# The first projected block of an MLP set in a fixed order on TensorE, VectorE and ScalarE

## The chip, the cores and the metric

One core of one Trainium2 chip runs the whole program. The metric is the device time of one execution in microseconds (us), as the median of several runs. TensorE (PE) multiplies matrices into PSUM, VectorE (DVE) and ScalarE (ACT) do the elementwise work and move results out of PSUM, and the queue of SyncE (SP) issues nearly all transfers.

## The reference

In short form (softmax(t, n) is over axis n). Three stages follow each other; the change lies at the beginning of the third. Attention with 48 heads gives x, a soft mixture of experts turns it into slots and combination weights, and an MLP follows:

```python
def _moe_ref(x, phi, w1, w2):
    logits = x @ phi                       # (1792, 32)
    slot_input = softmax(logits, 0).T @ x  # 32 slots of 768
    for e in range(8):
        slot_out[e] = relu(slot_input[e] @ w1[e]) @ w2[e]
    return softmax(logits, 1) @ slot_out

def _moe2_ref(x, w_in, w_out, alpha):
    h = x @ w_in                           # (1792, 768) @ (768, 2048)
    g = np.maximum(h, 0.0) + alpha * np.minimum(h, 0.0)
    return (g @ w_out).astype(np.float32)  # (1792, 2048) @ (2048, 768)
```

The arrays w_in and w_out come as float64, and the kernel turns them into float32 itself.

## The kernel before

Since the mixture's output is a combination of 32 slots, the kernel never forms it: it multiplies the 32 slot outputs (tile so) with w_in, which gives a_stk, and gets each hidden activation from a_stk and the combination weights (cstk) in one product. Numbers are kept in a high and a low part for TensorE's fast format; a part's product is taken three times (high by high, high by low, low by high).

The third stage begins when the last expert's product y stands in PSUM:

- `gather` (from L907) copies y out (ysb), transposes it (yt) and copies it twice into so. `idle` puts products of the identity (warm) where TensorE would have nothing to do.
- `a_block(fb, lo, w)` (from L925) makes columns of a_stk: 12 products in the two column halves of TensorE (aps), which the profile counts as 24, then for each half j a ScalarE copy of the high part (L950) and a VectorE subtraction for the low part (L951). Block 0 is made in two column blocks of 256 columns, the others whole.
- `hidden(tb, f)` (from L959) is the hidden row f of token block tb, 128 of the 2048 hidden units for 512 tokens: one product (hps, L962), two ReLUs on ScalarE (L968, L969), the weighted sum on VectorE (L970), the high part on ScalarE (L978) and the low part on VectorE (L979), in the tiles gs and gr. For the very first row VectorE does both halves of the activation itself (L974, L977).
- `to_single(f)` (from L816) converts row f of w_out from float64 to float32 with `to_f32` (L192): Abs on ScalarE (L194), then four operations on VectorE (L195, L199, L202, L205). `split_wo(f)` (from L826) splits it into high (ScalarE, L837) and low part (VectorE, L838), the tile wsp.
- `project(tb, f, tiles)` (from L994) multiplies a hidden row with its row of w_out into six PSUM banks: 24 products for a block of 512 tokens, 12 of them 512 wide and 12 256 wide (L1002, L1008, L1009; tile oc).

A main loop goes over 16 rows f for token block 0, then for block 1, and the four other blocks come after it in another form. Every engine runs its instructions strictly in the order in which they stand. That order is not the order of the code: a scheduler orders them by priorities and modelled times, and a manual dependency without a semaphore ("NOSYNC") only forces one instruction to stand behind another. PSUM tiles ps_w have two buffers, ps_c six. All transfers of weights stand in one queue in the order of their use.

```python
            hidden_to(1)
            idle(2, warm)
            hidden_to(2)
            a_block(0, 256, 128)

            for n, (tb, f) in enumerate(units):
                ...
                hidden_to(n + 3)
                ...
                project(tb, f, range(blocks[tb][1] // 128))
```

## Time and profile before

| | us |
|---|---|
| median of 3 runs | 587.15 |
| the three runs | 588.32, 585.62, 587.15 |
| the profiled execution | 587.28 |
| its span, first to last instruction | 585.0 |
| PE busy in the span | 553.1 (95%) |
| DVE busy | 435.1 (74%) |
| ACT busy | 377.6 (65%) |

The profile's page gives busy times for the whole span. The change concerns the stretch from about 327 us, where the last expert ends, to about 345 us, and through the order of the instructions the 100 us behind it. Times inside the span are counted from its first instruction. Consecutive matmuls overlap in the profile, so that the distance from start to start is what one costs, not its duration.

### The profile page before, as it was taken

What the parts mean: (1) busy time and instruction counts of PE and PEld (TensorE: products, weight loads), DVE (VectorE), ACT (ScalarE), POOL (GpSimd) and SP (SyncE); (2) the same over time, 40 slices, a digit from 0 to 9 for tenths busy, and PEclk for the clock granted to TensorE, in tenths of its full rate; (3) what the DMA queues carried; (4) which work ended last, traced back from release to release, by engine and by line L of the source; (5) the groups of instructions that cost most, each with busy time, mean ns of one, the idle gap of its engine ahead of it and who ended that gap; (6) DMA issues with size and microseconds to landing.
All of it is one profiled execution on the core that took longest, in us unless ns stands there. A gap on an engine that the chain in (4) does not pass through costs nothing.

```text
span 585.0 us, 10832 instructions
## 1 busy us (share of the span) xinstructions
PE 553.1 (95%) x4030; PEld 384.7 (66%) x4030; DVE 435.1 (74%) x834; ACT 377.6 (65%) x617; POOL 173.9 (30%) x158
## 2 busy tenths in 40 slices
PE   5999999999999999998888799999999999999996
PEld 4444444445444545464445577878888999999996
DVE  3878777796999768460023489999999979797974
ACT  3999999898889788530011266854777755555551
POOL 0789788676785755500000000000000000000000
PEclk9999999999999999999999999999999999999999
DMA  7668789987787971999999999200120101010101
GB/s 174 155 141 251 230 263 269 266 255 200 225 256 214 326 229 53 350 347 418 416 417 419 390 404 414 111 1 1 55 55 1 55 1 54 2 55 0 55 2 54
DMA packets 83460, 110.92 MB, mean 190 GB/s; under 512 B 55376, under 2 KB 63312, under 8 KB 81872
## 3 DMA queue, kind: packets, MB, share of 16 engines
q1 hardware_dynamic: 81168, 109.28, 55.3%
q10 hardware_dynamic: 2240, 0.95, 0.6%
q8 instruction: 32, 0.52, 0.4%
q14 instruction: 20, 0.16, 0.1%
HBM read 98.41 MB, written 11.80 MB: 188 GB/s over the span
## 4 chain that ended last, share of the span: by engine, by line
PE 71%; DMA 14%; ACT 8%; DVE 5%; issue 2%; SPq 1%; ACTq 0%
PE o L295 10%; DMA w<-in_moe_w_dram 9%; PE s L295 8%; PE P L1229 7%; PE P L1227 7%; PE P L1228 7%; PE oc L1002 6%; PE oc L1008 6%; PE oc L1009 6%; DMA v<-in_v_dram 3%; ACT p L398 2%; PE aps L930 2%; ACT p L397 2%; PE nx L295 2%; PE rs L295 2%
## 5 line engine op out<-in xcount | busy, mean ns | idle before, releaser
L295 PE MATMUL o<-p,v 128*64 128x448 f32 (+1 forms) x384 | 93.3, 564 | 5.8 <-ACT xu L423 3.7
L397 ACT ACTIVATE p<-s 128x896 f32<-128x896 f32 x96 | 78.7, 821 | 21.1 <-PE s L295 18.0
L398 ACT ACTIVATE p<-p,cap 128x896 f32<-128x896 f32 x96 | 90.9, 949 | 2.3
L414 POOL TENSOR_TENSOR acc<-p 128x448 f32<-128x448 f32 x48 | 62.1, 1313 | 55.6 <-ACT p L398 55.6
L1008 PE MATMUL oc<-wsp,gr 128*128 128x512 f32 (+1 forms) x192 | 65.3, 341 | 0.0
L1009 PE MATMUL oc<-wsp,gr 128*128 128x512 f32 (+1 forms) x192 | 64.1, 337 | 0.0
L1002 PE MATMUL oc<-wsp,gr 128*128 128x512 f32 (+1 forms) x192 | 62.6, 343 | 0.0
L295 PEld LDWEIGHTS s<-qh,kh 64*128 64x128 f32 (+1 forms) x168 | 18.1, 185 | 66.5 <-issue 25.6
L1218 ACT ACTIVATE gr<-gs 128x384 fp32r<-128x384 f32 (+1 forms) x64 | 36.7, 576 | 32.8 <-DVE gs L1202 26.9
L417 POOL TENSOR_TENSOR acc<-acc,p 64x448 f32<-64x448 f32 x46 | 55.4, 1204 | 1.7
L421 POOL TENSOR_TENSOR acc<-acc,p 128x448 f32<-128x448 f32 x46 | 53.5, 1183 | 1.8
L1219 DVE TENSOR_TENSOR gr<-gs,gr 128x384 fp32r<-128x384 f32 x64 | 39.2, 620 | 17.4 <-ACT gr L1218 17.4
L295 PE MATMUL s<-qh,kh 64*128 64x448 f32 (+1 forms) x168 | 45.8, 473 | 0.0
L1227 PE MATMUL P<-wsp,gr 128*128 128x384 f32 x128 | 42.9, 335 | 0.0
L1229 PE MATMUL P<-wsp,gr 128*128 128x384 f32 x128 | 42.8, 334 | 0.0
L1228 PE MATMUL P<-wsp,gr 128*128 128x384 f32 x128 | 42.8, 334 | 0.0
L1002 PEld LDWEIGHTS oc<-wsp,gr 128*128 128x128 f32 x192 | 36.6, 192 | 5.6 <-ACT wsp L837 0.8
L1008 PEld LDWEIGHTS oc<-wsp,gr 128*128 128x128 f32 x192 | 36.8, 191 | 5.2 <-DVE wx L205 0.4
L1009 PEld LDWEIGHTS oc<-wsp,gr 128*128 128x128 f32 x192 | 36.3, 189 | 4.4 <-issue 0.4
L295 PEld LDWEIGHTS o<-p,v 128*64 128x64 f32 (+1 forms) x384 | 19.0, 134 | 30.3 <-ACT xu L423 12.3
L295 PE MATMUL s<-ql,kh 64*128 64x448 f32 (+1 forms) x168 | 35.5, 366 | 1.0 <-DVE ql L377 1.0
L295 PE MATMUL s<-qh,kl 64*128 64x448 f32 (+1 forms) x168 | 35.5, 365 | 0.0
(237 smaller groups left out, 1227.3 us busy)
## 6 DMA issues: line engine op xcount, KB each, us to landing
w<-in_moe_w_dram SPq DMA_DIRECT2D x26, 768.0 KB, 12.4
w<-in_moe_w_dram SPq DMA_DIRECT2D x12, 1536.0 KB, 12.2
cvbuf<-in_moe_w_in_dram SPq DMA_DIRECT2D x24, 512.0 KB, 5.4
w<-in_moe_w_out_dram SPq DMA_DIRECT2D x16, 768.0 KB, 11.1
w_in<-cvbuf SPq DMA_DIRECT2D x24, 256.0 KB, 2.8
w<-in_moe_w_dram SPq DMA_DIRECT2D x12, 512.0 KB, 7.4
q<-in_q_dram SPq DMA_DIRECT2D x44, 112.0 KB, 3.6
k<-in_k_dram SPq DMA_DIRECT2D x48, 96.0 KB, 4.8
```

The costliest lines, as they stand in the source:

```text
L295: ins = nc.tensor.matmul(*a, **kw)
L397: nc.scalar.activation(out=pe, in_=ps[:, :n, :S], func=AF.Tanh)
L398: nc.scalar.activation(out=pe, in_=pe, func=AF.Exp, scale=cap_sb)
L414: nc.gpsimd.tensor_add(out=a[:, u, :], in0=pt[i, 0][:, u, :], in1=pe[:, u, :])
L417: nc.gpsimd.tensor_add(out=a[r, u, :], in0=a[r, u, :], in1=pt[i, JK][r, 0, :])
L421: nc.gpsimd.tensor_add(out=a[:, u, :], in0=a[:, u, :], in1=pe[:, u, :])
L1002: ins = nc.tensor.matmul(o, gh[:, ts], wo_h[f][:, cols], start=(f == 0 and not second), stop=False)
L1008: nc.tensor.matmul(o, gh[:, ts], wo_l[f][:, cols], start=False, stop=False)
L1009: nc.tensor.matmul(o, gl[:, ts], wo_h[f][:, cols], start=False, stop=(f == KF - 1 and not more))
L1227: nc.tensor.matmul(o, hi[:, i], bh, start=(p == 0), stop=False)
L1228: nc.tensor.matmul(o, hi[:, i], bl, start=False, stop=False)
L1229: nc.tensor.matmul(o, lo[:, i], bh, start=False, stop=(p == 7))
```

## The change

The first block of the third stage gets a fixed order on three engines. A function `follow` chains instructions of ScalarE ("a") and VectorE ("v") to each other, and the matmuls of the block are chained by `pe[0]`.

- Copies in `gather` are divided: VectorE takes the first half of ysb and of so, ScalarE the second.
- `to_f32` ends after the shift; the two last operations are `to_f32_end`. For row 1 of w_out the first part comes ahead of the first column block's copies, the second part behind the first hidden row's activation.
- The first hidden row (`hidden_0`) has a PSUM buffer of its own from ps_c. Its 512 tokens are divided in two halves of 256: VectorE works on the first, ScalarE's two ReLUs on the second. Its low part (`low_0`) follows later, in two halves.
- The second column block's products come right behind the first hidden row's product, its copies (`late_copies`) behind everything of hidden row 1 and of the split of row 1 of w_out.
- `project_0` does the first row's projection in another order and chained behind the matmul that was written before it, which is that of hidden row 2.
- Six warm products of the identity become three.

```diff
-        def to_single(f):
+        def follow(lane, ins, yes=True):
+            if not yes:
+                return ins
+            if lane in turn:
+                tc.add_manual_dep(ins.ins, turn[lane].ins.name, NOSYNC, reason="first block in a fixed order")
+            turn[lane] = ins
+            return ins
+
+        def to_single(f, first=False):
...
-            nc.vector.tensor_copy(out=ysb, in_=yacc[:32 * G3, :256])
+            follow("v", nc.vector.tensor_copy(out=ysb[:, :128], in_=yacc[:32 * G3, :128]))
+            follow("a", nc.scalar.activation(out=ysb[:, 128:], in_=yacc[:32 * G3, 128:256], func=AF.Copy))
...
+                if lo and first:
+                    return copy_out
+                copy_out()
...
+            def hidden_0():
...
+                follow("a", a.activation(out=mn[:, y], in_=ps[:, y], func=AF.Relu, scale=-1.0))
+                follow("v", v.tensor_scalar(
+                    out=mn[:, x], in0=ps[:, x], scalar1=0.0, scalar2=al, op0=ALU.min, op1=ALU.mult
+                ))
+                follow("a", a.activation(out=gf[:, y], in_=ps[:, y], func=AF.Relu))
+                follow("v", v.scalar_tensor_tensor(
+                    out=gf[:, x], in0=ps[:, x], scalar=0.0, in1=mn[:, x], op0=ALU.max, op1=ALU.add
+                ))
+                follow("a", a.activation(out=gh[:, x], in_=gf[:, x], func=AF.Copy))
+                follow("v", v.scalar_tensor_tensor(
+                    out=gf[:, y], in0=mn[:, y], scalar=na, in1=gf[:, y], op0=ALU.mult, op1=ALU.add
+                ))
+                follow("a", a.activation(out=gh[:, y], in_=gf[:, y], func=AF.Copy))
...
+            def project_0():
+                gh, gl = gt[0, 0]
+                for left, right in ((gh, (wo_h[0], wo_l[0])), (gl, (wo_h[0],))):
...
+                                tc.add_manual_dep(
+                                    ins.ins, pe[0].ins.name, NOSYNC, reason="first block in a fixed order"
+                                )
+                                pe[0] = ins
...
-            to_single(1)
-            split_wo(1)
-            a_block(0, 0, 128)
-            idle(4, warm)
...
+            first, then, shift = to_single(1, True)
+            follow("a", first)
+            follow("v", then)
+            follow("v", shift)
+            a_block(0, 0, 128, True)
+            idle(3, warm)
+            hidden_0()
+            late_copies = a_block(0, 256, 128, True)
+            for ins in to_f32_end(where["wo", 0, 0][:, 1], wf[0][1]):
+                follow("v", ins)
+            low_0()
+            steps = hidden(0, 1, True)
+            for _ in range(3):
+                next(steps)
+            split_wo(1, True)
+            for _ in steps:
+                pass
+            late_copies()
+            ready[0] = 2
...
-                project(tb, f, range(blocks[tb][1] // 128))
+                if n == 0:
+                    project_0()
+                else:
+                    project(tb, f, range(blocks[tb][1] // 128))
```

**ScalarE and VectorE from the first column block to the copies of the second.** A wait is named by the engine or the transfer queue (DMAHW) whose semaphore it is on. ScalarE before:

```order
L950 ACTIVATE a_stk<-aps 64x128 [waits DMAHW0_49,DMAHW7_49,PE_49,Pool_49]
L194 ACTIVATE wf<-w 128x768 [waits DMAHW4_49]
L950 ACTIVATE a_stk<-aps 64x128 [waits DVE_49]
L968 ACTIVATE gs<-hps 128x512 [waits DMAHW7_49,DMAHW0_49,PE_49]
L969 ACTIVATE gs<-hps 128x512
```

ScalarE now:

```order
L936 ACTIVATE ysb<-y 96x128 [waits DVE_49]
L947 ACTIVATE so<-yt 128x2x3x32 [waits DMAHW5_49,DVE_49,Pool_49]
L194 ACTIVATE wf<-w 128x768 [waits DMAHW4_49]
L958 ACTIVATE a_stk<-aps 64x128 [waits DMAHW7_49,DMAHW0_49,PE_49]
L958 ACTIVATE a_stk<-aps 64x128 [waits DVE_49]
L1029 ACTIVATE gs<-hps 128x256 [waits DMAHW7_49,DMAHW0_49,PE_49]
L1033 ACTIVATE gs<-hps 128x256 [waits DVE_49]
L1037 ACTIVATE gr<-gs 128x256 [waits DMAHW6_49,DMAHW5_49,DVE_49]
L1041 ACTIVATE gr<-gs 128x256 [waits DVE_49]
```

VectorE's L1030 and L1034, in the same stretch, wait for ScalarE's semaphore in turn. VectorE before, from the first subtraction for a_stk:

```order
L951 TENSOR_TENSOR a_stk<-aps,a_stk 64x128
L974 TENSOR_SCALAR gs<-hps,alpha 128x512
L195 TENSOR_SCALAR wf<-wf 128x768
L951 TENSOR_TENSOR a_stk<-aps,a_stk 64x128
L199 TENSOR_SCALAR wf<-wf 128x768
L977 SCALAR_TENSOR_TENSOR gs<-hps,gs 128x512
L202 SCALAR_TENSOR_TENSOR wf<-w,wf 128x768
L970 SCALAR_TENSOR_TENSOR gs<-gs,nalpha 128x512
L205 SCALAR_TENSOR_TENSOR wf<-w,wf 128x768
L979 TENSOR_TENSOR gr<-gs,gr 128x512 x2
L951 TENSOR_TENSOR a_stk<-aps,a_stk 64x128
```

VectorE now, from behind its copy into so:

```order
L195 TENSOR_SCALAR wf<-wf 128x768
L199 TENSOR_SCALAR wf<-wf 128x768
L959 TENSOR_TENSOR a_stk<-aps,a_stk 64x128 x2
L1030 TENSOR_SCALAR gs<-hps,alpha 128x256
L1034 SCALAR_TENSOR_TENSOR gs<-hps,gs 128x256
L1038 SCALAR_TENSOR_TENSOR gs<-gs,nalpha 128x256
L207 SCALAR_TENSOR_TENSOR wf<-w,wf 128x768
L210 SCALAR_TENSOR_TENSOR wf<-w,wf 128x768
L1048 TENSOR_TENSOR gr<-gs,gr 128x256 x2
L1012 SCALAR_TENSOR_TENSOR gs<-gs,nalpha 128x512
L859 TENSOR_TENSOR wsp<-wf,wsp 128x768
L1016 TENSOR_TENSOR gr<-gs,gr 128x512
```

The next VectorE row now is the pair of subtractions for the second column block. Row 1's Abs and its first two VectorE operations moved ahead of the first column block's copies, and the second column block's subtractions moved behind the split of row 1.

**TensorE from the first column block to the first projection.** Before:

```order
L930 MATMUL aps<-w,so 64x128 x12
L812 MATMUL warm<-ident 128x128 x4
L962 MATMUL hps<-cstk,a_stk 128x512
L812 MATMUL warm<-ident 128x128 x2
L962 MATMUL hps<-cstk,a_stk 128x512
L930 MATMUL aps<-w,so 64x128 x12
L1002 MATMUL oc<-wsp,gr 128x512
L1008 MATMUL oc<-wsp,gr 128x512
```

Nine more projection matmuls follow before the next hps, that of hidden row 2. Now:

```order
L965 MATMUL aps<-w,so 64x128 x12
L820 MATMUL warm<-ident 128x128 x3
L1022 MATMUL hps<-cstk,a_stk 128x512
L965 MATMUL aps<-w,so 64x128 x12
L1002 MATMUL hps<-cstk,a_stk 128x512 x2
L1058 MATMUL oc<-wsp,gr 128x512 x2
L1058 MATMUL oc<-wsp,gr 128x256 x2
```

The product of hidden row 2 (the second of the two hps) now stands ahead of all 24 projection matmuls, where 11 of them stood ahead of it.

**TensorE at column block 1 of a_stk** (the same is seen at blocks 2 and 3). Before:

```order
L930 MATMUL aps<-w,so 64x256 x8
L962 MATMUL hps<-cstk,a_stk 128x512
L930 MATMUL aps<-w,so 64x256 x2
L1002 MATMUL oc<-wsp,gr 128x512
L1008 MATMUL oc<-wsp,gr 128x512
L930 MATMUL aps<-w,so 64x256 x2
L1009 MATMUL oc<-wsp,gr 128x512
```

Now:

```order
L1058 MATMUL oc<-wsp,gr 128x512
L1058 MATMUL oc<-wsp,gr 128x256
L965 MATMUL aps<-w,so 64x256 x12
L1002 MATMUL hps<-cstk,a_stk 128x512
L1086 MATMUL oc<-wsp,gr 128x512
```

The 12 products of the block, which stood in three pieces between others, now stand together.

## Rows read from the trace of the kernel before

**Rows 1.** TensorE in order of time: start, duration, line, output<-inputs, count, idle before.
```profile
331.32 0.47 PE L962 MATMUL hps<-cstk,a_stk 128*128 128x512 f32 x1
...
334.74 2.16 PE L930 MATMUL aps<-w,so 128*64 128x128 f32 x24 [0.82 <-DVE gs L977]
336.83 0.80 PE L1002 MATMUL oc<-wsp,gr 128*128 128x512 f32 x1
...
340.38 0.39 PE L962 MATMUL hps<-cstk,a_stk 128*128 128x512 f32 x1
340.61 0.39 PE L1009 MATMUL oc<-wsp,gr 128*128 128x512 f32 x1
...
342.03 0.28 PE L1008 MATMUL oc<-wsp,gr 128*128 128x256 f32 x1
342.15 0.28 PE L1009 MATMUL oc<-wsp,gr 128*128 128x256 f32 x1
```

**Rows 2.** Stretches: length; busy PE, PEld, DVE, ACT, POOL; granted clock, DMA share, GB/s.
```profile
335.00:336.00 1.00, 1.00 (x18) 1.00 (x16) 1.00 (x2) 0.57 (x2) 0.00 (x0) 0.74 1.01 385
336.00:337.00 1.00, 1.00 (x11) 0.67 (x8) 1.00 (x2) 0.69 (x2) 0.00 (x0) 0.50 1.04 383
...
338.00:339.00 1.00, 1.00 (x4) 0.80 (x3) 0.94 (x3) 0.97 (x4) 0.00 (x0) 0.55 1.03 391
...
430.00:440.00 10.00, 10.00 (x62) 8.89 (x61) 9.91 (x22) 7.65 (x19) 0.00 (x0) 1.00 0.00 0
```

**Rows 3.** ScalarE in order of time, from the first column block.
```profile
330.56 0.27 ACT L950 ACTIVATE a_stk<-aps 64x128 fp32r<-64x128 f32 x1 [9.33 <-PE aps L930]
330.73 0.90 ACT L194 ACTIVATE wf<-w 128x768 f32<-128x768 f32 x1
```

**Rows 4.** VectorE in order of time, in the same stretch.
```profile
327.32 0.42 DVE L911 COPY ysb<-y 96x256 f32<-96x256 f32 x1 [5.29 <-PE y L893]
...
332.50 0.55 DVE L195 TENSOR_SCALAR wf<-wf 128x768 f32<-128x768 f32 x1
...
339.11 0.95 DVE L838 TENSOR_TENSOR wsp<-wf,wsp 128x768 fp32r<-128x768 f32 x1
340.10 0.29 DVE L951 TENSOR_TENSOR a_stk<-aps,a_stk 64x128 fp32r<-64x128 f32 x1
```

**Rows 5.** The transfer of row 1 of w_out: its issue, and the median from issue to landing.
```profile
314.86 3.61 SPq L172 DMA_DIRECT2D w<-in_moe_w_out_dram  x1
...
w<-in_moe_w_out_dram SPq DMA_DIRECT2D x1, 768.0 KB, 15.5
```

**Rows 6.** Groups by form, 326 to 460 us: count | busy, mean ns | idle before.
```profile
L970 DVE SCALAR_TENSOR_TENSOR gs<-gs,nalpha 128x512 f32<-128x512 f32 x15 | 11.2, 745 | 0.1
L970 DVE SCALAR_TENSOR_TENSOR gs<-gs,nalpha 128x256 f32<-128x256 f32 x16 | 7.7, 479 | 0.0
L979 DVE TENSOR_TENSOR gr<-gs,gr 128x256 fp32r<-128x256 f32 x16 | 6.7, 419 | 0.0
L968 ACT ACTIVATE gs<-hps 128x256 f32<-128x256 f32 x16 | 6.0, 376 | 1.3 <-PE hps L962 1.3
```

**Rows 7.** TensorE in order of time at column blocks 1 and 2 of a_stk.
```profile
342.36 1.95 PE L930 MATMUL aps<-w,so 128*64 128x256 f32 x16
344.24 0.50 PE L962 MATMUL hps<-cstk,a_stk 128*128 128x512 f32 x1
344.67 0.65 PE L930 MATMUL aps<-w,so 128*64 128x256 f32 x4
345.25 0.50 PE L1002 MATMUL oc<-wsp,gr 128*128 128x512 f32 x1
...
350.33 0.40 PE L962 MATMUL hps<-cstk,a_stk 128*128 128x512 f32 x1
...
359.14 0.39 PE L962 MATMUL hps<-cstk,a_stk 128*128 128x512 f32 x1
...
367.51 0.50 PE L962 MATMUL hps<-cstk,a_stk 128*128 128x512 f32 x1
```

More of the change, by code (lines that the diff above doesn't have):

```diff
@@ L823, in to_single, with split_wo @@
             wf.setdefault(i, []).append(t)
-            to_f32(where["wo", 0, i][:, kk], t)
-        def split_wo(f):
+            ins = to_f32(where["wo", 0, i][:, kk], t)
+            if not first:
+                to_f32_end(where["wo", 0, i][:, kk], t)
+            return ins
+        def split_wo(f, first=False):
             i, kk = divmod(f, 2)
@@ L937, in a_block @@
                         )
+                        if lo or first:
+                            tc.add_manual_dep(ins.ins, pe[0].ins.name, NOSYNC, reason="first block in a fixed order")
+                        pe[0] = ins
                 if lo + 2 * w == 512:
@@ L957, in mlp, with hidden @@
             gt, accs = {}, {}
-            def hidden(tb, f):
+            def hidden(tb, f, first=False):
                 t0, w = blocks[tb]
                 ps = ps_w.tile([128, 512], F32, tag="w", name="hps")[:, :w]
-                pe[0] = nc.tensor.matmul(ps, a_stk[:, f * 128:(f + 1) * 128], cstk[:, t0:t0 + w], start=True, stop=True)
+                ins = nc.tensor.matmul(ps, a_stk[:, f * 128:(f + 1) * 128], cstk[:, t0:t0 + w], start=True, stop=True)
+                if first:
+                    tc.add_manual_dep(ins.ins, pe[0].ins.name, NOSYNC, reason="first block in a fixed order")
+                pe[0] = ins
                 o = 512 * (f % 4)
@@ new lines, in hidden @@
+                yield follow("a", nc.scalar.activation(out=gh, in_=gf, func=AF.Copy), first)
+                yield follow("v", nc.vector.tensor_sub(out=gl, in0=gf, in1=gh), first)
+                gt[tb, f] = (gh, gl)
+            def hidden_0():
+                w, h = blocks[0][1], blocks[0][1] // 2
+                ps = ps_c.tile([128, 512], F32, tag="c", name="hps")[:, :w]
+                ins = nc.tensor.matmul(ps, a_stk[:, 0:128], cstk[:, 0:w], start=True, stop=True)
+                tc.add_manual_dep(ins.ins, pe[0].ins.name, NOSYNC, reason="first block in a fixed order")
+                pe[0] = ins
+                gh, gl, mn, gf = gr[:, 0:w], gr[:, 2048:2048 + w], gs[:, 0:w], gs[:, 2 * w:3 * w]
+                x, y = slice(0, h), slice(h, w)
+                al, na = alpha_sb[:, 0:1], nalpha_sb[:, 0:1]
+                v, a = nc.vector, nc.scalar
+                follow("a", a.activation(out=mn[:, y], in_=ps[:, y], func=AF.Relu, scale=-1.0))
[11 more added lines that the diff above has]
+                follow("a", a.activation(out=gh[:, y], in_=gf[:, y], func=AF.Copy))
+                gt[0, 0] = (gh, gl)
@@ new lines, in low_0 @@
+            def low_0():
+                w = blocks[0][1]
+                (gh, gl), gf = gt[0, 0], gs[:, 2 * w:3 * w]
+                for part in (slice(0, w // 2), slice(w // 2, w)):
+                    follow("v", nc.vector.tensor_sub(out=gl[:, part], in0=gf[:, part], in1=gh[:, part]))
+            def project_0():
+                gh, gl = gt[0, 0]
+                for left, right in ((gh, (wo_h[0], wo_l[0])), (gl, (wo_h[0],))):
+                    for s in range(blocks[0][1] // 128):
+                        ts = slice(128 * s, 128 * s + 128)
+                        for c, cols in enumerate(COLS):
+                            for m, b in enumerate(right):
+                                start = left is gh and m == 0 and not (c == 1 and s % 2 == 1)
+                                ins = nc.tensor.matmul(
+                                    accs[0, s][c], left[:, ts], b[:, cols], start=start, stop=False
+                                )
+                                tc.add_manual_dep(
+                                    ins.ins, pe[0].ins.name, NOSYNC, reason="first block in a fixed order"
+                                )
+                                pe[0] = ins
```

72 lines of the change are left out of this document (41 added, 31 removed).

## Prediction

> **What bounds the kernel now.** I read the page's slices first: TensorE is at nine tenths or more in nearly all of the second half, with a dent where the third stage begins. Then TensorE's instructions in order of time around that dent. The last expert ends at 327.3 us, when VectorE's copy of y begins [rows 4], and from 336.83 us on TensorE projects and has no idle time before any row again [rows 1, 7]. From there to the end its work is the bound: what the change does to the finish is the time at which TensorE ends a given matmul, as long as the others keep up. Between 327 and 336.8 us the bound is a chain over three engines: copies of y, first column block, its two copies, first hidden row. VectorE is busy 9.91 of 10 us as late as 430 to 440 us [rows 2], so it is a second bound close below TensorE's. The granted clock is the third thing to see: it is at half (1.2 GHz) from about 335.5 to 338.9 us, after TensorE had waited twice, and costs 0.26 + 0.5 + 0.5 + 0.45 = 1.7 us of work there [rows 2] (the third of these four stretches reads like the second).
>
> The sum is made on the profiled execution, 587.28 us (span 585.0), which stands 0.13 us above the median of 587.15.
>
> **Gather.** Halving the copies looks like a gain on the path. But ScalarE's half waits for VectorE's in the new order, so the halves follow each other. A copy of y 256 wide takes 0.42 us [rows 4]; VectorE's half is some 0.28 us (an estimate from the step of 256 elements between 745 and 479 ns [rows 6]), ScalarE's 0.27 us, as its copy 128 wide [rows 3]. That is 0.13 us longer with a hop between engines of some 0.04; the first transposition starts earlier in exchange. Same again for so. I take +0.1 us, with 0 and +0.3 as ends.
>
> **Row 1's Abs ahead of the first copies.** The transfer of row 1 of w_out lands at 314.86 + 15.5 = 330.36 us [rows 5]. The first column block is done at 330.5, when ScalarE's copy starts today [rows 3]. The new order puts Abs (0.90 us [rows 3]) ahead of this copy on ScalarE and clip and shift (0.55 us each [rows 4]) ahead of the subtraction on VectorE. So: Abs 330.4 to 331.3, clip and shift to 332.45, subtraction to 332.7, first hidden product at 332.8 instead of 331.32 [rows 1]: +1.5 us, the 0.1 of the gather hidden in it. Queued behind the Abs are both copies of the block and, through them, the first hidden row.
>
> **First hidden row in halves.** Both engines read one PSUM tile, and the order makes them alternate: ReLU on ScalarE, minimum on VectorE, ReLU, maximum. With 376 ns for a ReLU 256 wide and 479 ns for a VectorE operation 256 wide (nearest row; the true forms may be 0.05 us off either way) [rows 6], the product's 0.47 us and four hops, the fourth ends at 332.8 + 0.47 + 2 x 0.38 + 2 x 0.48 + 0.16 = 335.2 us. Side by side it would end near 334.25. This is the place where a rule of the Trainium skill speaks against the change: "PSUM — Partial Sum Buffer", section "PSUM bank collisions raise a hardware error", says that two engines must not touch the same PSUM bank and 32 partitions at once, two readers included, and that the compiler's scheduler therefore sets a dependency between them. By that rule halves of one tile gain nothing by sharing, and the waits in the order agree; without it the sum below would be some 0.9 us lower. No run here shows what happens without the waits.
>
> **What stands ahead of the second column block's copies.** VectorE then has, up to the first of the two late subtractions: third piece of row 0 (0.48), the two last operations of row 1's conversion (0.95 each), two low parts (0.42 each), row 1's weighted sum (0.75), the split's low part (0.95), row 1's low part (0.69, as in the two of 512 that it replaces), the subtraction (0.29) [rows 4, 6]. That is 5.9 us; independent operations overlap by some 0.08 each, eight times, so 5.3 us: it ends at 340.45, and the product of hidden row 2 starts at 340.5. Today it starts at 340.38 [rows 1]. VectorE has thus lost nothing, but TensorE has: all 24 projection matmuls now stand behind this product, and 11 of them ran ahead of it today. TensorE has its second column block and row 1's product from about 333.1 to 335.3 us and then nothing for 5 us. Bounds of this chain: 0.6 us either way (twelve operations, 0.05 each).
>
> **The first projection.** Behind 340.5 us come the product and 24 matmuls: 13 at 0.23 and 12 at 0.12 us from start to start [rows 1], 4.4 us at full clock. After 5 us of nothing I take the clock to be at half at 340.5. Before, full clock came back at 338.9, 4.2 us after TensorE had taken up work at 334.74 [rows 1, 2], and the loss was 1.7 us; half clock for all of 4.2 us would be 2.1. I take 2.0, ends 0 and 2.1. The first projection ends at 346.9 instead of 342.27 (342.15 + 0.12 [rows 1]): **+4.6 us**, of which 2.5 are the 11 matmuls and 2.0 the clock. The warm products given up stand in idle time and count nothing by themselves.
>
> **Column blocks 1 to 3 in one piece.** This is the side of the change that the diff doesn't show. A row of the main loop takes 4.4 us by the count above. From 359.14 to 367.51 us there are one row and column block 2: 8.37 us, so 3.97 us for the block; for block 1, 350.33 − 342.27 − 4.4 = 3.66 us [rows 1, 7]. A piece of 16 takes 1.88 us, one of 4 takes 0.58 [rows 7]: 0.108 us each and 0.15 per piece, so 24 in one piece are 2.75 us, 2.95 with the slower start of the neighbours (345.25 to its follower and the matmul before a piece lose 0.1 each). Saved: 0.7 + 1.0, and 1.0 for block 3, which stands in three pieces as well: **−2.7 us**, ends −1.5 and −3.2. Cover: TensorE works without idle time there, so the saving counts in full, provided that VectorE and ScalarE are in time; they lead more than before, since TensorE comes 4.6 us later.
>
> **Later waits.** The rows of token block 1 leave VectorE 0.1 us in ten [rows 2], and its order changed; I take +0.2 us, ends 0 and +2.
>
> Sum: +4.6 − 2.7 + 0.2 = +2.1, so 587.28 + 2.1 = **589.4 us**. About 0.5% (2.9 us, so 584.2 to 590.1) is what a measurement of this kernel can tell from no change.
>
> **Rivals.** (1) *The clock costs nothing*, because TensorE isn't throttled after the wait or recovers at once: −2.0, so 587.4 us. Against it: half clock followed waits of about 2 us in all before. 12%. (2) *Row 1's transfer is early*, by 1.5 us or more, and Abs, clip and shift fall into the time of the first column block: the chain starts at 331.4, everything to 340.5 comes 1.4 us earlier: 588.0 us. For it: transfers are back to back and their pace may vary; against: the queue ahead is the same. 13%. (3) *VectorE takes over as the bound*, the slower side: what TensorE saves in blocks 1 to 3 brings it up to VectorE, which has 9.91 of 10 us of work and starts no earlier than before; then none of the 2.7 us is won: 587.28 + 4.6 = 591.9 us. It decides if VectorE's low parts come later than TensorE's need of them, from about 420 us. 20%. (4) *The faster side*: the project's wait isn't there, because VectorE gets to the late subtractions before 336.5 us; then half clock and pieces are both saved, −1.7 − 2.7: 582.9 us. That needs the chain 4 us shorter than the sum of its rows. 5%. The forecast has 50%.
>
> **How the numbers follow.** The forecast with its bounds lies between 588 and 591, mostly within 0.5%: of its 50 I give 9 to slower. With (3), slower has 9 + 18 = 0.27, faster 0.05, same 0.68. The range is 587.0 to 592.0: (1) to (3) are in it, outside are (4) and the ends of the chain that add up.
>
> **What would show it.** Right: in the profile after, the product of row 2 at 340 to 341 us with TensorE idle some 5 us before it; granted clock at half around 341 to 344; the first projection's end near 347; the distance from one hps to the next over a column block 7.3 us instead of 8.37; no idle time before oc rows later. Wrong: Abs before 330 us (2), a clock of 1.00 from 340 on (1), waits of oc for VectorE's low parts behind 420 us (3), the projection starting before 338 us (4).

## The result and the profile after

| | before | after |
|---|---|---|
| median, us | 586.43 (4 runs) | 590.68 (4 runs) |
| range, us | 585.62 to 588.32 | 590.18 to 590.88 |
| profiled execution, us | 587.28 | 590.88 |
| its span | 585.0 | 589.1 |

The ratio of after to before is 1.0064, with a 95% interval from 1.0044 to 1.0084: slower by 2.6 to 4.9 us. In the table of the experiments, two medians each contain one execution far above all others (1004 us for the first projection behind hidden row 1, 1814 us for Abs later), which the ratios leave out. The forecast was 589.4 us, with 587.0 to 592.0 as its range. The time lies in the range, but the step from before to after, 3.75 us, is larger than the +2.1 us of the sum, and the sum turns out to have been made of partly wrong terms.

Since the first two stages end at another time in each execution, times behind them are counted from the end of the last y product and written y+. In the profiled execution of before y ends at 327.26 us, in that of after at 325.03 + 3.65 = 328.68 us. TensorE of after in order of time (start, duration, line, output<-inputs, count, idle time before the row and who ended it):

```profile
325.03 3.65 PE L917 MATMUL y<-w,small 128*32 128x256 f32 x48 [0.35 <-DVE small L910]
...
334.20 0.49 PE L1022 MATMUL hps<-cstk,a_stk 128*128 128x512 f32 x1 [1.25 <-DVE a_stk L959]
...
336.09 0.50 PE L1002 MATMUL hps<-cstk,a_stk 128*128 128x512 f32 x1
341.94 0.80 PE L1002 MATMUL hps<-cstk,a_stk 128*128 128x512 f32 x1 [5.35 <-DVE a_stk L959]
342.53 5.43 PE L1058 MATMUL oc<-wsp,gr 128*128 128x512 f32 x24
347.90 2.81 PE L965 MATMUL aps<-w,so 128*64 128x256 f32 x24
350.64 0.50 PE L1002 MATMUL hps<-cstk,a_stk 128*128 128x512 f32 x1
...
583.39 0.34 PE L1313 MATMUL P<-wsp,gr 128*128 128x384 f32 x1
```

They answer to [rows 1, 7]. The first hidden product stands at y+5.52 (before y+4.06), that of row 2 at y+13.26 (before y+13.12), ahead of it TensorE is idle for 5.35 us, and the first projection ends where column block 1 starts, at y+19.22 (before y+15.1). The block then takes 350.64 − 347.90 = 2.74 us in one piece. The last matmul stands at y+254.71 instead of y+252.21. So 2.5 of the 3.6 us between the two profiled executions lie behind y, 1.42 ahead of it, and −0.3 behind the last matmul.

Behind the wait the clock is at half. Stretches of after (length; busy PE, PEld, DVE, ACT, POOL; granted clock, DMA share, GB/s):

```profile
336.00:341.00 5.00, 0.59 (x5) 0.19 (x1) 4.88 (x9) 3.47 (x8) 0.00 (x0) 1.00 1.04 395
341.00:342.00 1.00, 0.06 (x1) 0.06 (x1) 0.85 (x2) 0.08 (x1) 0.00 (x0) 0.72 1.06 430
342.00:343.00 1.00, 1.00 (x3) 0.81 (x4) 0.29 (x1) 1.00 (x3) 0.00 (x0) 0.50 1.01 399
...
344.00:345.00 1.00, 1.00 (x6) 0.81 (x5) 1.00 (x3) 1.00 (x3) 0.00 (x0) 0.58 1.00 401
345.00:346.00 1.00, 1.00 (x8) 0.86 (x7) 1.00 (x3) 0.76 (x1) 0.00 (x0) 1.00 1.03 424
```

They answer to [rows 2]: TensorE is busy for 0.59 of 5 us, then comes half clock (1.2 GHz), and 2.4 GHz is back at 345. Up to here the trace reads as the prediction said. One thing does not. Some 100 us later VectorE waits for ScalarE's ReLUs (L1011), and 9 us after that TensorE waits for VectorE's low part. VectorE of after, ScalarE, and then TensorE:

```profile
429.42 0.49 DVE L1012 SCALAR_TENSOR_TENSOR gs<-gs,nalpha 128x256 f32<-128x256 f32 x1 [0.88 <-ACT gs L1011]
430.39 0.43 DVE L1016 TENSOR_TENSOR gr<-gs,gr 128x256 fp32r<-128x256 f32 x1 [0.48 <-ACT gr L1015]
431.70 0.48 DVE L1012 SCALAR_TENSOR_TENSOR gs<-gs,nalpha 128x256 f32<-128x256 f32 x1 [0.88 <-ACT gs L1011]
```

```profile
427.66 0.42 ACT L1015 ACTIVATE gr<-gs 128x256 fp32r<-128x256 f32 x1 [0.74 <-DVE gs L1012]
427.98 0.85 ACT L1099 ACTIVATE ob<-oc 128x512 f32<-128x512 f32 x2
428.72 0.39 ACT L1010 ACTIVATE gs<-hps 128x256 f32<-128x256 f32 x1
```

```profile
441.58 0.50 PE L1093 MATMUL oc<-wsp,gr 128*128 128x512 f32 x1 [0.29 <-DVE gr L1016]
```

ScalarE isn't held up by TensorE directly: it makes the ReLU at 428.72 us from a product that TensorE had begun at 426.93 us, because it had itself waited for VectorE (0.74 us, and 0.55 us a row later) and then copied out two banks of the finished token block. The wait of 0.29 us costs more than itself: the row's matmuls around it take 0.86 us more than without a wait (3.08 us from one product of a hidden row to the next, 2.22 elsewhere). In before neither VectorE nor TensorE waits there.

### The profile page after: what moved, and what is told of

It reads as the page before. It is cut to its first block, busy times and chain, and to the rows that moved or that the text cites. A ratio compares the mean times of both kernels' runs of the same rounds, so it can differ in the third digit from the quotient of the medians.

```text
span 589.1 us, 10829 instructions
## 1 busy us (share of the span) xinstructions
PE 552.5 (94%) x4024; PEld 384.6 (65%) x4024; DVE 435.2 (74%) x835; ACT 378.3 (64%) x622; POOL 174.0 (30%) x158
## 4 chain that ended last, share of the span: by engine, by line
PE 69%; DVE 10%; DMA 9%; ACT 8%; issue 3%; SPq 1%; ACTq 0%; DVEq 0%
PE o L301 10%; PE s L301 9%; PE P L1313 6%; PE P L1311 6%; PE P L1312 6%; PE oc L1093 4%; PE oc L1086 4%; PE oc L1092 3%; PE h L893 3%; PE y L917 3%; DMA w<-in_moe_w_out_dram 3%; DMA w<-in_moe_w_dram 2%; PE nx L301 2%; PE rs L301 2%; ACT p L404 2%
## 5 line engine op out<-in xcount | busy, mean ns | idle before, releaser
L1093 PE MATMUL oc<-wsp,gr 128*128 128x512 f32 (+1 forms) x184 | 62.0, 337 | 0.3 <-DVE gr L1016 0.3
L1086 PE MATMUL oc<-wsp,gr 128*128 128x512 f32 (+1 forms) x184 | 62.1, 338 | 0.0
L1092 PE MATMUL oc<-wsp,gr 128*128 128x512 f32 (+1 forms) x184 | 62.0, 337 | 0.0
L1093 PEld LDWEIGHTS oc<-wsp,gr 128*128 128x128 f32 x184 | 34.8, 189 | 4.8 <-DVE gr L1016 0.9
L1092 PEld LDWEIGHTS oc<-wsp,gr 128*128 128x128 f32 x184 | 34.9, 190 | 4.3
L1086 PEld LDWEIGHTS oc<-wsp,gr 128*128 128x128 f32 x184 | 34.9, 190 | 3.9 <-ACT gr L1015 0.2
```

What stands on the lines that cost most here:

```text
L1086: ins = nc.tensor.matmul(o, gh[:, ts], wo_h[f][:, cols], start=(f == 0 and not second), stop=False)
L1092: nc.tensor.matmul(o, gh[:, ts], wo_l[f][:, cols], start=False, stop=False)
L1093: nc.tensor.matmul(o, gl[:, ts], wo_h[f][:, cols], start=False, stop=(f == KF - 1 and not more))
```

## The experiments

Two theories stand against each other. **By TensorE**: what TensorE waits or loses behind y adds up to the end, since it has no idle time there; this is the prediction's way of summing. **By VectorE**: VectorE is as much of a bound over the next 100 us, so what counts is its idle time, and a gain of TensorE alone is given back in waits for VectorE. All runs in one table; "VectorE idle" is 130 us less its busy time between y and y+130, "end" the start of the last matmul; both are of the profiled execution. The ratios come from runs of before made at the same time as the kernel's, and need not be the quotient of two medians of the table.

| kernel | VectorE idle, us | end | median, us | ratio to before (95%) |
|---|---|---|---|---|
| before | 6.31 | y+252.21 | 586.43 | |
| before, again | 6.32 | y+252.31 | 589.37 (1 run) | |
| before, as its own control | 4.81 | y+250.74 | 586.48 | 1.0001 (0.9976 to 1.0026) |
| after | 9.00 | y+254.71 | 590.68 | 1.0064 (1.0044 to 1.0084) |
| after, again | 8.26 | y+254.10 | 590.50 | 1.0067 (1.0043 to 1.0090) |
| first projection behind hidden row 1 | 8.40 | y+253.83 | 589.42 | 1.0052 (1.0032 to 1.0072) |
| 14 warm products in the wait | 8.04 | y+253.24 | 589.02 | 1.0044 (1.0024 to 1.0063) |
| first hidden row in two banks | 8.44 | y+254.17 | 588.75 | 1.0049 (1.0033 to 1.0066) |
| Abs later | 10.08 | y+255.85 | 591.80 | 1.0065 (1.0041 to 1.0090) |
| before, blocks whole | 4.90 | y+250.45 | 586.29 | 1.0003 (0.9983 to 1.0022) |
| three edits joined | 6.07 | y+251.39 | 586.60 | 0.9999 (0.9979 to 1.0018) |
| the same, no sign operation | 13.16 | y+248.01 | 582.93 | 0.9917 (0.9888 to 0.9946) |
| before, blocks whole, low parts on GpSimd | 11.58 | y+267.62 | 603.49 | 1.0303 (1.0280 to 1.0326) |
| joined but one bank, low parts on GpSimd | 16.70 | y+270.25 | 604.99 | 1.0326 (1.0308 to 1.0344) |

In the eleven executions with the same VectorE work, the end less VectorE's idle time lies between 245.2 and 246.0 us, while the ends themselves differ by 5.4 us. That is one reading of the table: what the order does to the end shows in VectorE's idle time. It is an account, not yet a cause, since VectorE can also be idle because TensorE is late.

### After and before once more

> The changed kernel once more, against the kernel before. In its profiled execution the last expert ended 1.4 us later than in that of before, although every engine's instructions up to there stand in the same order. Theory: these 1.4 us belong to the single execution, so the end of y varies by about 1 us here too, and what the change costs behind y is 4.1 (first projection) - 3.0 (blocks whole) + 1.4 (later waits) = 2.5 us: ratio near 1.0045. Rival: the first stage is slower in this build; then y ends at 328.5 us or later again and the ratio stays at 1.0064 or above.

> The kernel before once more. Counted from the end of y, its trace should repeat: product of hidden row 2 at 13.1 us, last matmul at 252.2 us, both within 0.3 us; the end of y itself lies anywhere from 327 to 331 us, as in the five executions seen so far. Rival: behind y, too, executions differ by 1 us or more; then a difference of 2 us between two traces is not read from one execution each.

> The kernel before against itself, in as many rounds as the others: what the comparison gives where nothing differs. Theory: 1.000 with an interval of 0.002 on either side, and the end of y in its trace between 325.7 and 331 us, 252.3 us ahead of the last matmul. If it comes out at 1.002 or above, a part of the changed kernel's 1.0064 to 1.0067 is of that kind, because the traces show only 1.9 to 2.5 us of its 3.8 us behind y.

Nothing is edited. The end of y stood at 328.92 us for after, at 329.69 and 327.25 us for before; over fourteen executions of all the kernels, in which everything ahead of it stands in one order, it lies between 325.70 and 330.99 us. So one profiled execution can't price the 1.42 us ahead of y. But my theory that they are all of the excess fell too: the ratio of after stayed at 1.0067. Both signs of the rival, a slower first stage, came: y at 328.92 us, and the ratio. The other executions speak against it: y ends at 328.7 us on average in the five executions of before and its variants, and at 327.9 us in the nine of after and its variants. And the control brought what one trace can't show: from y to the last matmul it takes 250.74 us, 1.5 us less than in the other two executions of the same kernel. TensorE of the control, and its clock in two of the stretches that [rows 2] show at 0.74 and 0.50:

```profile
333.42 0.49 PE L962 MATMUL hps<-cstk,a_stk 128*128 128x512 f32 x1 [1.19 <-DVE a_stk L951]
334.73 1.53 PE L930 MATMUL aps<-w,so 128*64 128x128 f32 x24 [0.82 <-DVE gs L977]
...
338.84 0.39 PE L962 MATMUL hps<-cstk,a_stk 128*128 128x512 f32 x1
```

```profile
335.00:336.00 1.00, 1.00 (x24) 1.00 (x20) 1.00 (x2) 0.56 (x2) 0.00 (x0) 1.00 1.02 385
336.00:337.00 1.00, 1.00 (x10) 0.70 (x7) 1.00 (x3) 0.76 (x3) 0.00 (x0) 1.00 1.05 387
```

The two waits right ahead are the same to 0.01 us (start 333.42 and 334.73; in before the same two products start at 333.43 and 334.74), and yet the clock stays at 2.4 GHz. The product of row 2 stands at y+11.59 instead of y+13.12.

Further ahead the two executions do differ, which neither the prediction nor my reading of [rows 2] took in. In the last expert TensorE of before waited twice for weights; TensorE of the control did not, but had half clock some 66 us ahead of y. TensorE of before and its stretch from 261 us, then the same of the control:

```profile
324.24 1.06 PE L893 MATMUL y<-w,small 128*32 128x256 f32 x12 [0.23 <-DMA w<-in_moe_w_dram]
326.20 1.06 PE L893 MATMUL y<-w,small 128*32 128x256 f32 x12 [0.90 <-DMA w<-in_moe_w_dram]
261.00:264.70 3.70, 3.44 (x55) 2.02 (x54) 2.05 (x8) 0.45 (x2) 0.31 (x1) 1.00 1.03 404
```

```profile
323.37 3.88 PE L893 MATMUL y<-w,small 128*32 128x256 f32 x48 [0.35 <-DVE small L886]
261.00:264.70 3.70, 3.70 (x40) 1.98 (x44) 2.05 (x8) 0.31 (x1) 0.31 (x1) 0.54 1.03 407
```

The second execution of before waits like the first (0.63 and 0.91 us) and has the half clock behind y. The kernels "blocks whole" and "blocks whole, low parts on GpSimd", whose first 13 us behind y stand in the order of before, are like the control in both. So of five executions the two with these waits for weights lost the clock behind y, and the three without did not. The rows go together; no run changed one to see the other.

Where the clock is at half behind y, VectorE feels it as well: with row 2 late, VectorE has nothing to do for 1.50 us. VectorE of before in the first profiled execution; the control has the same instruction without this wait:

```profile
347.55 0.69 DVE L979 TENSOR_TENSOR gr<-gs,gr 128x512 fp32r<-128x512 f32 x1 [1.50 <-ACT gr L978]
```

Against the control, after is 3.97 us longer behind y (3.36 in its second execution); against the first execution 2.50. The measured 0.0064 of 586.4 are 3.75 us. How often before keeps the full clock behind y isn't shown: three executions have a trace, two with half clock there and one without. What causes it is open beyond what goes together above.

The second execution of after shows a rival of the prediction at work. Row 1 of w_out had landed before it was wanted, Abs started at y+1.86 instead of y+3.05, and the first hidden product stood at y+4.34 instead of y+5.52. The product of row 2 came 1.17 us earlier too (y+12.09). At the end 0.6 of these 1.2 us were left. By TensorE nothing was left: half clock lasted 6.8 us there against 3.4 in the first execution, and column block 1 starts at y+19.18 against y+19.22. VectorE's idle time is 0.74 us less.

### The first projection behind hidden row 1

```diff
             late_copies()
             ready[0] = 2
+            anchor = pe[0]
 ...
                 if n == 0:
+                    pe[0] = anchor
                     project_0()
```

> The changed kernel, but the first projection is chained behind the product of hidden row 1 and no longer behind that of hidden row 2. Theory: the wait of 5.35 us and the half clock behind it go; the first projection ends some 14.5 us after y instead of 19.2, and the time falls by 4 to 5 us against the changed kernel, to a ratio of 0.998 against the kernel before. Column blocks 2 and 3 stand in two or three pieces in this order, which gives back 0.3 to 0.6 us. Rival: VectorE is the bound there (9.9 of 10 us busy); then TensorE waits for low parts between 345 and 440 us, and the gain is under 2.5 us, a ratio above 1.002.

The wait went: the projection starts at y+8.36, and behind its 24 matmuls, five of the next row and the product of row 2, column block 1 starts at y+14.16 instead of y+19.22, at full clock. Yet the end came only 0.3 to 0.9 us earlier, and the ratio is 1.0052. TensorE of this kernel:

```profile
335.65 4.47 PE L1058 MATMUL oc<-wsp,gr 128*128 128x512 f32 x24 [0.43 <-ACT gr L1037]
...
341.45 2.81 PE L965 MATMUL aps<-w,so 128*64 128x256 f32 x24
...
349.07 0.47 PE L1002 MATMUL hps<-cstk,a_stk 128*128 128x512 f32 x1 [1.35 <-DVE a_stk L959]
...
351.10 0.50 PE L1092 MATMUL oc<-wsp,gr 128*128 128x512 f32 x1 [0.42 <-DVE wsp L859]
```

Eight us after the gain the first waits for VectorE stand there, one for the subtraction of a column block, one for a low part of w_out. Two more, of 0.63 and 0.35 us, stand at the change to token block 1, and column blocks 2 and 3 stand in pieces. Against the first execution of after VectorE's idle time fell by 0.6 us and the end by 0.9, against the second VectorE idles 0.1 us more and the end is 0.3 earlier. My theory of 4 to 5 us fell, and the rival, a gain under 2.5 us because VectorE is a bound, came true.

### Column blocks whole, in the kernel before

In `a_block` the first product is chained behind the last projection matmul written before it, and hidden and projection products behind the block's last:

```diff
+                        if fb and kk == j == 0:
+                            behind(pe[0], last_oc[0])
 ...
+                behind(pe[0], last_aps[0])
```

> The kernel before, with one edit: the products of column blocks 1, 2 and 3 stand together, nothing else of TensorE between them. Theory: each piece more costs TensorE about 0.3 us, the distance over a block falls from 8.37 to 7.25 us and the time by 2.5 to 3.0 us, a ratio of 0.995. Rival: VectorE is the bound of the first token block; then TensorE waits for its low parts, and the ratio is 0.998 to 1.001.

This is the term of −2.7 us alone. The distance over block 2 fell from 8.37 to 8.07 us only, since one of its neighbours now waits, that over block 3 is 8.45 us, and the end stands at y+250.45. Against the control, which also ran at full clock behind y, that is 0.3 us, and the ratio is 1.0003, as the rival had it. Where it went:

```profile
362.02 1.42 PE L1014 MATMUL oc<-wsp,gr 128*128 128x512 f32 x6 [0.57 <-ACT wsp L837]
...
384.93 0.50 PE L1021 MATMUL oc<-wsp,gr 128*128 128x512 f32 x1 [0.56 <-DVE wsp L838]
```

What TensorE lost in pieces before, it loses here around waits for VectorE and ScalarE. Whole blocks are no gain by themselves.

### The wait filled with warm products

```diff
             late_copies()
             ready[0] = 2
+            idle(14, warm)
```

> The changed kernel with 14 more products of the identity between the products of hidden rows 1 and 2, where TensorE waits for 5.35 us. Theory: the half clock from 341.7 us on comes from this wait; with it filled, the granted clock is 1.00 at the first projection, its 24 matmuls take 4.2 us instead of 5.4 and the product of row 2 0.23 instead of 0.59: 1.5 us less than the changed kernel. Rival: the clock falls for another reason; then the projection keeps its 5.4 us and the time stays.

The product of row 2 stands at the same y+13.28, the projection behind it takes 345.27 − 340.96 = 4.31 us instead of 5.37, and the end falls from y+254.71 to y+253.24: 1.47 us, as expected. TensorE waited for 2.23 us more behind the warm products, and the clock stayed at 1.00 in each stretch:

```profile
341.00:342.00 1.00, 1.00 (x7) 0.86 (x6) 0.50 (x2) 1.00 (x2) 0.00 (x0) 1.00 1.01 412
342.00:343.00 1.00, 1.00 (x8) 0.87 (x7) 0.96 (x3) 0.97 (x3) 0.00 (x0) 1.00 1.00 414
```

So the half clock in after is the price of the empty wait, 1.5 us, and 14 warm products in that place are worth as much. This is the one gain of TensorE alone that reached the end in full: in after TensorE comes 4 us late, and VectorE's idle time falls with it, by 1.0 us.

### The first hidden row in two banks

```diff
-                ps = ps_c.tile([128, 512], F32, tag="c", name="hps")[:, :w]
+                pa = ps_c.tile([128, 512], F32, tag="c", name="hps")[:, :w]
+                pb = ps_c.tile([128, 512], F32, tag="c", name="hps")[:, :w]
```

ScalarE reads its half from pb, VectorE its own from pa; each is made by a product 256 wide.

> The changed kernel, but the first hidden row's product is made in two PSUM banks, one for VectorE's half and one for ScalarE's. Theory: the halves alternated only because they read one bank; now they run side by side, VectorE's waits of 0.37 and 0.45 us there go, the product of row 2 comes 12.4 us after y instead of 13.26, and the end 0.8 us earlier: ratio 1.004 to 1.005. Rival: something else makes them take turns; then 13.26 us and a ratio of 1.006 stay.

In after ScalarE and VectorE take turns, in four steps, each waiting for the other (first ScalarE, then VectorE):

```profile
334.73 0.38 ACT L1029 ACTIVATE gs<-hps 128x256 f32<-128x256 f32 x1 [0.28 <-PE hps L1022]
335.67 0.38 ACT L1033 ACTIVATE gs<-hps 128x256 f32<-128x256 f32 x1 [0.55 <-DVE gs L1030]
```

```profile
335.15 0.48 DVE L1030 TENSOR_SCALAR gs<-hps,alpha 128x256 f32<-128x256 f32 x1 [0.37 <-ACT gs L1029]
336.08 0.42 DVE L1034 SCALAR_TENSOR_TENSOR gs<-hps,gs 128x256 f32<-128x256 f32 x1 [0.45 <-ACT gs L1033]
```

With two banks both run side by side (ScalarE, then VectorE):

```profile
331.67 0.39 ACT L1031 ACTIVATE gs<-hps 128x256 f32<-128x256 f32 x1 [0.17 <-PE hps L1024]
331.95 0.38 ACT L1035 ACTIVATE gs<-hps 128x256 f32<-128x256 f32 x1
```

```profile
331.86 0.48 DVE L1032 TENSOR_SCALAR gs<-hps,alpha 128x256 f32<-128x256 f32 x1
332.38 0.42 DVE L1036 SCALAR_TENSOR_TENSOR gs<-hps,gs 128x256 f32<-128x256 f32 x1
```

The product of row 2 moved from y+13.26 to y+12.53, 0.73 us, and the end by 0.54 us instead of the 0.8 expected. So the waits came from the shared tile, which is one bank; tile and bank changed together, so that the run doesn't tell one from the other. The Trainium skill, "PSUM — Partial Sum Buffer", section "PSUM bank collisions raise a hardware error", which the prediction's step on the halves drew on, says that the compiler's scheduler sets a dependency between instructions of two engines that touch the same bank and 32 partitions. The trace agrees, with 0.73 us as the price here.

TensorE doesn't bring this gain to the end. Half clock lasted 6.8 us in this execution against 3.4 in after (the granted clock from row 2's product to column block 1 is 0.62 against 0.76 on average), so that column block 1 starts at y+19.57, 0.35 us later than in after. The end is earlier all the same, and VectorE's idle time is 0.56 us less.

### Abs later

```diff
-            first, then, shift = to_single(1, True)
-            follow("a", first)
-            follow("v", then)
-            follow("v", shift)
             a_block(0, 0, 128, True)
             idle(3, warm)
             hidden_0()
+            behind(to_single(1, True))
```

> The changed kernel, but Abs, clip and shift of row 1 of w_out stand behind the first hidden row's activation and not ahead of the first column block's copies. What the prediction's step says: the first hidden product comes 1.4 us earlier, 4.1 us after y. Theory by the traces since: that gains nothing at the end, since VectorE's chain sets the product of row 2, and VectorE now waits for Abs behind ScalarE's last copy: row 2 at 14.2 us after y instead of 13.26, the last matmul at 255.5 instead of 254.7 (or 254.1 where the row lands early). Rival: TensorE's chain counts, everything moves 1.4 us forward: row 2 at 11.9 us, last matmul at 253.3.

The first hidden product moved forward by 1.4 us, to y+4.09, and everything behind it moved back: row 2 at y+14.38, the end at y+255.85. VectorE of this kernel, between the first hidden row and row 1's conversion:

```profile
336.31 0.47 DVE L1038 SCALAR_TENSOR_TENSOR gs<-gs,nalpha 128x256 f32<-128x256 f32 x1
338.04 0.56 DVE L195 TENSOR_SCALAR wf<-wf 128x768 f32<-128x768 f32 x1 [1.26 <-ACT wf L194]
```

VectorE waits 1.26 us for Abs, which now stands behind ScalarE's last copy of the first hidden row. The 1.5 us that the prediction booked as a cost of "Abs first" are real at that product, but this order doesn't win them back. It doesn't show that they are worth nothing: in the second execution of after, where the row landed 1.2 us earlier, 0.6 us reached the end. The ratio, 1.0065, is that of after.

### VectorE with less to do

The first of two kernels joins the edits of three runs above (`anchor`, whole blocks, two banks). The second leaves the sign out, too, for the rows from 2 on:

```diff
+        if not sign:
+            return (low,)
         sign = nc.vector.scalar_tensor_tensor(
```

> The changed kernel with three edits at once: first projection chained behind hidden row 1, column blocks whole, first hidden row in two PSUM banks. Theory: both engines are bounds, VectorE has the same work as before in this stretch, and its waits in the first 13 us are some 0.6 us longer than before and 0.7 shorter than in the changed kernel; so the end lies near that of the kernel before with whole blocks: last matmul 250 to 251.5 us after y, ratio 0.996 to 1.000. Rival: TensorE alone is the bound; then 1.2 us of earlier start and 3 us of whole blocks add up, 248 us.

> The same three edits, and the last operation of the conversion (the sign, 0.95 us on VectorE) is left out for rows 2 to 15 of w_out, 13 us of VectorE's work. Theory: VectorE is the second bound, so TensorE's waits for it go and the last matmul stands 1.5 to 2.5 us earlier than with the three edits alone, 248 to 249.5 us after y. Rival: TensorE alone is the bound; then the time is that of the three edits within 0.3 us.

The three edits above in one kernel give an end at y+251.39 and a ratio of 0.9999: 3.3 us better than after, no better than before. Leaving out one VectorE operation for 14 rows moves the end by 3.4 us, to y+248.01, which is more than the 1.5 to 2.5 I expected. The stretch from y to y+130 (columns as above) in the control, in after and in the kernel without the sign operation:

```profile
327.25:457.25 130.00, 127.92 (x774) 107.22 (x774) 125.19 (x219) 88.95 (x178) 0.00 (x0) 1.00 0.39 147
```

```profile
328.68:458.68 130.00, 122.91 (x746) 104.05 (x746) 121.00 (x209) 85.82 (x174) 0.00 (x0) 0.99 0.38 144
```

```profile
327.83:457.83 130.00, 127.84 (x788) 109.33 (x787) 116.84 (x213) 93.55 (x188) 0.00 (x0) 1.00 0.40 150
```

VectorE is busy for 125 of 130 us in the control, against 121 in after. Without the sign it is busy for 117, and TensorE's 1.9 us of idle time between y+23 and y+90 (with the three edits alone) are gone. That settles that VectorE is a bound of this stretch. It isn't the only one: 13 us of its work were taken away, 3.4 us came back, and TensorE has no wait left behind y+23.

The two bounds also hang together. Where TensorE makes the products of rows 0 and 1 of token block 1 some 4 to 5 us apart, VectorE's idle time from y+90 to y+110 grows with TensorE's lateness, read at the product of the last row of token block 0: 0.54 us in before with blocks whole (y+77.64), 1.50 with the wait filled (y+79.73), 2.32 in after (y+80.80), 2.42 with Abs later (y+82.13). After once more (y+80.77) and two banks (y+81.16) have 2.31 and 2.32. Where the two products follow each other directly, as in before, it is 0.18 us. So the traces speak for a part of VectorE's idle time being TensorE's lateness, come back through the order at the change of blocks; no run tests it by itself.

### The low parts on GpSimd

```diff
-            nc.vector.tensor_sub(out=both[:, 1], in0=t, in1=both[:, 0])
+            (nc.gpsimd if f >= 2 else nc.vector).tensor_sub(out=both[:, 1], in0=t, in1=both[:, 0])
```

> The kernel before with column blocks 1 to 3 whole, and besides the low parts of the rows 2 to 15 of w_out (0.95 us each on VectorE) on GpSimd, which is idle there. Theory: VectorE is the second bound; with 13 us of its work gone TensorE's waits for it (0.1 + 0.6 + 0.7 us with whole blocks alone) go, and the last matmul stands 249.1 us after y, against 250.45 with whole blocks alone and 252.2 before: ratio 0.995 to 0.997. Rival: GpSimd is late itself or slows VectorE down; then 250.4 us or more and a ratio of 1.000.

> The changed kernel with the first projection chained behind hidden row 1, the column blocks whole, and the low parts of rows 2 to 15 of w_out on GpSimd. Theory: the first projection starts 8.4 us after y and not 13.9, and what the first of these edits alone did not bring (its gain of 5 us at column block 1 was gone 7 us later, when TensorE waited for VectorE) now stays: last matmul 248 to 249.5 us after y, against 254.7 and 253.8; ratio 0.993 to 0.996 against the kernel before. Rival: TensorE's waits in the first rows are for the conversions themselves, which remain on VectorE; then 251 us or more.

Both are 17 to 19 us slower than before, far more than the rivals had, of which the first named the reason, GpSimd late or in VectorE's way. So they say nothing on the bound. What they show stands in the last section.

## Why the prediction was right, and where it was not

**Gather** (+0.1): from the end of y to the first column block 1.87 us instead of 1.68: +0.19, inside its bounds.

**Abs ahead of the first copies** (+1.5 at the first hidden product): +1.46, on the spot, and for the reason given: Abs waits for the row's transfer until y+3.05. The landing is on the path to row 2, since row 2 came 1.17 us earlier where the row landed 1.2 us earlier. But the place of Abs isn't free to choose: with Abs later VectorE waits for it 1.26 us, as the prediction's own step on the second column block lets one expect, where VectorE's queue sets the time.

**Second column block's copies** (row 2 at 340.5 us, which is y+13.24): y+13.26, and TensorE idle for 5.35 us ahead of it, as said.

**First projection** (+4.6): it ended at y+19.22 instead of y+15.1, so +4.1. The clock cost 1.5 instead of 2.0: 0.36 us for row 2's product (0.59 instead of 0.23 to its follower) and 1.1 for the 24 matmuls (5.37 us instead of the 4.3 with the wait filled).

**Column blocks whole** (−2.7): the distances over blocks 1, 2 and 3 change by −0.72, −1.13 and −1.13 us, so −3.0. As a term of TensorE it was right. As a gain it was wrong to count it "in full": alone it brought 0.3 us. In after it appears without a wait of TensorE, which comes 4 us late there; that VectorE's lead is the reason is argued from the run with blocks whole, not shown by itself.

**Later waits** (+0.2, ends 0 and +2): the term that was mis-sized behind y. The prediction took it from VectorE's 0.1 us in ten [rows 2], without rows of the order behind, and its sign "no idle time before oc rows later" failed. It is +1.4: in span times the product of the last row of token block 0 stands at 409.49 us instead of 406.95, 2.5 us later, and the last matmul 3.9 us later. Of these 1.4 us the wait at 440 us is 0.86. VectorE had 2.2 us without work from y+100 to y+110, where before had 0.1, and was late afterwards. With it goes an order that the sum left out: the products of rows 0 and 1 of token block 1, which follow each other in before, are 4.3 us apart in after. No run changed this order alone. TensorE of before, then of after:

```profile
411.36 0.40 PE L962 MATMUL hps<-cstk,a_stk 128*128 128x256 f32 x2
```

```profile
413.89 0.28 PE L1002 MATMUL hps<-cstk,a_stk 128*128 128x256 f32 x1
...
418.19 0.28 PE L1002 MATMUL hps<-cstk,a_stk 128*128 128x256 f32 x1
```

Rival (3), VectorE as the bound, had 20%; its sign, a wait of oc for a low part behind 420 us, came, and VectorE as a second bound is what the runs show, though "no gain of the 2.7" was the wrong price for it.

**The base.** The sum was made on an execution of before with half clock from 335.5 to 338.9 us, and took this 1.7 us as a property of the kernel. The control ran without. Rival (1), "the clock costs nothing", I considered for after alone, never for before, and the reason against it, half clock behind waits of about 2 us, fell with the control. This is the step that failed, and it would explain most of the gap between +2.1 and the measured +3.75: against an execution of before at full clock behind y, the measured terms add up to +3.97 instead of +2.5. That most of the timed executions of before ran so isn't shown.

That the time lies in the range is in part luck. Between the first two traces the measured terms, +4.1 − 3.0 + 1.4 = +2.5, come near the sum of +2.1 because two terms that came out 0.5 and 0.3 us lower hide most of the third, 1.2 us higher.

Summed by VectorE, the change is shorter to tell. Against the control, VectorE idles 4.2 us more: 0.5 up to y+6, 0.7 from y+6 to y+13 (the halves that take turns), 0.7 from y+13 to y+23 (0.34 for ScalarE's copy of the second column block, 0.50 for the Abs of a later row, less 0.15 in the control), 2.1 from y+100 to y+110 (where TensorE's lateness seems to come back), 0.2 elsewhere. The end comes 3.97 us later.

What stays open: how often before runs at full clock behind y, and so how much of the 3.75 us is the 1.5 of its clock; what decides where the half clock falls; and whether the time ahead of y takes any part, for which the averages of y above give no sign.

## What to carry to other kernels

Where two engines are busy for 95% or more of the same 100 us, as TensorE and VectorE are in before, sum the idle time of both from the trace before pricing an edit: here the end followed VectorE's idle time within 0.8 us over eleven executions, and TensorE's savings of 3 and 5 us came back as waits, while 1.5 us came through where TensorE was the late one. A fixed order for the first 15 us has to be judged by which engine it leaves without work, not by how early the first product stands. And before a sum is made on one profiled execution, a second one of the same kernel shows which of its losses repeat.

## What the runs showed of the hardware

The granted clock does not follow from the two waits right ahead alone. Behind the same waits of 1.19 and 0.82 us, TensorE of before went to 1.2 GHz for 3.4 us in two executions and stayed at 2.4 GHz in the third, worth 1.5 us at the end. The two had waits for weights of 0.2 to 0.9 us in the last expert as well; the third had none, and its half clock of 3.4 us stood some 66 us ahead of y. This goes together in all fourteen traces: eight have half clock there and no such waits, six have the waits and no half clock there. In every kernel with an empty wait of 4.6 to 7.8 us ahead of row 2 (both traces of after, two banks, Abs later) half clock followed, for 3.4 us once and 6.8 us three times.

VectorE loses time while GpSimd works. With the low parts on GpSimd, a subtraction of 128x768 took 2.59 us there on average (1.84 to 5.20) against 0.95 on VectorE, and several of VectorE's own operations grew: the weighted sum 512 wide from 746 to 1390 ns on average, single ones to 2.34 us. Others did not (L205 has 951 and 950 ns). How fast GpSimd is beside an idle VectorE, no run shows. The groups of the stretch from 360 to 440 us (count | busy, mean ns | idle before), with whole blocks alone and then with GpSimd:

```profile
L982 DVE SCALAR_TENSOR_TENSOR gs<-gs,nalpha 128x512 f32<-128x512 f32 x11 | 8.2, 746 | 0.0
L202 DVE SCALAR_TENSOR_TENSOR wx<-w,wx 128x768 uint32<-128x768 uint32 x8 | 7.6, 953 | 0.1
```

```profile
L982 DVE SCALAR_TENSOR_TENSOR gs<-gs,nalpha 128x512 f32<-128x512 f32 x11 | 15.3, 1390 | 0.9 <-ACT gs L981 0.9
L202 DVE SCALAR_TENSOR_TENSOR wx<-w,wx 128x768 uint32<-128x768 uint32 x8 | 12.5, 1568 | 0.0
```

The Trainium skill, "SBUF — State Buffer", section "Who interferes with whom", says that the two engines share a pair of ports and that whoever holds it blocks the other for a whole instruction, an operation with two inputs in SBUF included. The traces agree in that both engines' operations are longer side by side: 17 us were lost for 13 us of work moved away. That the ports are the reason isn't shown.
